# Four scale groups instead of five, and one tile's norm moved earlier, in a one-core DiT block

## Chip, cores and metric

The kernel runs on one core of a Trainium2 chip. The metric is the device time of one execution in microseconds, lower is better. Engines are named as the profile names them: PE (matrix multiply), PEld (its weight loads), DVE (vector), ACT (scalar), POOL (general purpose), SP (the queue that issues most loads).

## The reference, cut to what matters

One block of a diffusion transformer: B=2, N=256 tokens, D=1152, all bf16.

```python
mod = (silu(c) @ w_mod).reshape(B, 6, 1, D)
shift_a, scale_a, gate_a, shift_m, scale_m, gate_m = [mod[:, i] for i in range(6)]
h   = layernorm(x) * (1 + scale_a) + shift_a
q, k, v = split(h @ wqkv)                      # 2 heads
x   = x + gate_a * (softmax(q k^T / sqrt(Dh)) v @ wo)
h2  = layernorm(x) * (1 + scale_m) + shift_m
out = x + gate_m * (gelu(h2 @ w_fc1) @ w_fc2)
```

The change touches only the first line of `h` and the K projection.

## The kernel before

The start is a race between loads and PE. One SP queue loads `x`, then, in turns, a group of columns of `w_scale_a` (the scale part of w_mod) and the rows of `w_k` that go with them. PE computes the scale of a chunk of 128 channels with nine small matmuls (`scale_group`), DVE adds one to it, PE transposes the normalized chunk, DVE modulates batch 0 and ACT batch 1 (`both`), and PE does the six K matmuls of that chunk (`k_step`).

```python
SGROUPS = [(0, 2), (2, 4), (4, 6), (6, 8), (8, 9)]
for k0, k1 in SGROUPS:
    nc.sync.dma_start(w_scale_a[:, :, k0*P:k1*P], wmod_v[:, :, S_SCALE_A*D + k0*P : S_SCALE_A*D + k1*P])
    for a, z in [(0, 1), (1, 2)] if k0 == 0 else [(k0, k1)]:
        load_k(a, z, 0, KM1 * P)
# ... cut ...
for k in range(3, KD):
    split = 2 if k == 5 else 0
    k_step(k, 0, T, 0, split)                          # the first `split` of six matmuls
    if k in (3, 5, 7):
        k1 = min(k + 3, KD)
        scale_add(scale_group(k + 1, k1), k + 1, k1)
    if k < KD - 1:
        both(transpose_x([k + 1], range(NT)), k + 1)   # transposes, then modulation of step k+1
    k_step(k, 0, T, split)                             # the rest
```

Two later places matter, and the change does not touch them. After the softmax, the loads of the next weights wait for the softmax's DMA transposes, because bulk loads slow such transposes down (in the kernel before, the transpose that is issued at 87.72 us behind the load block below lands 8.9 us later; in before_piece_later, with the last 864 KB of that block held back, 4.7 us later); meanwhile POOL's queue broadcasts `gate_a` to all partitions:

```python
# inside softmax / attention output, cut
    transposed = softmaxes[i]()             # ends in nc.scalar.dma_start_transpose(...)
    if i == 0: gate_a = gate_finish()       # two gpsimd.dma_start(..., partition_broadcast(P))
# ...
w_shift_m = load_rows("w_shift_m", wmod_v, S_SHIFT_M * D)
tc.add_manual_dep(first_load["w_shift_m"], transposed.ins.name, WAIT_FOR, reason="transposes first")
w_scale_m = load_rows(...);  w_f1[0] = load_rows(...)      # the load block: 8.85 MB
w_f1[1] = wide_tile("w_f1_1")                              # first 384 columns belong to the block,
for c0, c1 in ((0, PW), (PW, D)): load = nc.sync.dma_start(w_f1[1][:, :, c0:c1], ...)
w_f1_1_rest = load.ins                                     # the rest waits for batch 1's modulation
```

And the second layernorm turns its result with DMA transposes too (`hT<-xn`, one for each token tile); DVE and ACT then modulate `hT` in place (`ln2_modulate`), and the first MLP matmul reads it.

## Time and profile before

| | before |
|---|---|
| median of 3 runs (low to high) | 244.13 us (243.77 to 244.66) |
| span of the profiled run | 242.2 us |
| PE busy, clock | 98%, 1.0 |
| first scale matmul / first Q matmul / first MLP matmul | 9.24 / 32.77 / 98.01 us |

The page of the kernel before: the span, the packets of all DMA queues, and the chain of work that ended last, by engine.

```profile
span 242.2 us, 3991 instructions
...
DMA packets 48781, 53.29 MB, mean 220 GB/s; under 512 B 9587, under 2 KB 36475, under 8 KB 48763
...
PE 85%; SPq 8%; DMA 5%; issue 0%; DVE 0%; DVEq 0%
...
```

The same chain in order of time (start us, length us, what). This is the view that says what would have to be shorter.

```profile
...
20.32 12.40 DMA w_q<-in_wqkv_dram
...
32.77 5.35 PE pq L522 x24
...
89.30 8.88 PE pacc L691 x54
98.18 68.26 PE pacc L744 x423
...
```

Up to 32.72 us the chain hangs on the load of w_q, from 32.77 us on it is PE work alone. (The chain starts a piece where the one before has ended, and pipelined ends overlap, so it has 98.18 where the timeline below has the first MLP matmul at 98.01.)

The timeline of PE in the K phase (start us, length us, engine, line, operation, out<-in, shape, count, and in brackets the idle time before it and what ended it). The start of a matmul group says more than its length, because matmuls are pipelined.

```profile
...
9.24 0.60 PE L247 MATMUL pm<-sT,w_scale_a 128*128 128x2 bf16 x18 [0.46 <-DMA w_scale_a<-in_w_mod_dram]
...
12.20 0.81 PE L280 MATMUL pk<-big,w_k 128*128 128x256 bf16 x6 [0.44 <-DVE big L270]
12.85 0.59 PE L247 MATMUL pm<-sT,w_scale_a 128*128 128x2 bf16 x18
...
15.72 0.59 PE L247 MATMUL pm<-sT,w_scale_a 128*128 128x2 bf16 x18
...
16.39 1.46 PE L280 MATMUL pk<-big,w_k 128*128 128x512 bf16 x6
...
17.91 1.89 PE L280 MATMUL pk<-big,w_k 128*128 128x512 bf16 x8
...
32.77 5.35 PE L522 MATMUL pq<-hT,w_q 128*128 128x512 bf16 x24 [0.16 <-DMA w_q<-in_wqkv_dram]
...
```

9.24 is the first scale group, just landed. 12.20 is step 0's second half (batch 1), after 0.44 us of idle PE. 12.85 is the scale of chunks 2-3, 15.72 that of chunks 4-5, ahead of step 3 (16.39). Step 4 with two matmuls of step 5 starts at 17.91. From 12.20 to 29.7 us PE has no idle time.

### The profile page before, as it was taken

The page shows a single profiled execution, that of the slowest core. Times are in us where ns is not written, and L with a number is a line of the kernel's source. Part 1 is how long each engine was busy: PE and PEld are TensorE (multiplying, and loading weights), DVE is VectorE, ACT ScalarE, POOL GpSimd, SP SyncE. Part 2 cuts the span into 40 slices and gives each one's busy share as a digit, 9 for nine tenths or more (in the row PEclk, how much of TensorE's full clock was granted, in tenths as well). Part 3 has the DMA queues.
Part 4 walks back from the last instruction along what each step waited for, and adds up shares of the span by engine and source line. Part 5 has one row for each costly group of instructions (what it writes and reads, how often), then busy time and mean ns, then how long its engine had stood idle before and what let it go on. Part 6 is the DMA issues. An engine that isn't in the chain of part 4 may idle for free.

```text
span 242.2 us, 3991 instructions
## 1 busy us (share of the span) xinstructions
PE 236.7 (98%) x1699; PEld 144.9 (60%) x1699; DVE 91.2 (38%) x193; ACT 60.0 (25%) x121; POOL 28.1 (12%) x47
## 2 busy tenths in 40 slices
PE   8899999999999999999999999999999999999994
PEld 5685444465667665888844444444666566656674
DVE  4742442318316678831001999960010000000001
ACT  6633322307215032771422233322000000000000
POOL 2200000001300333200000000001121111111111
PEclk9999999999999999999999999999999999999999
DMA  6999999997579999239999999999300000000000
GB/s 210 318 317 294 378 367 391 389 392 241 124 252 399 387 382 182 47 58 334 392 390 392 345 326 302 273 326 289 94 20 16 20 16 16 19 18 17 27 23 16
DMA packets 48781, 53.29 MB, mean 220 GB/s; under 512 B 9587, under 2 KB 36475, under 8 KB 48763
## 3 DMA queue, kind: packets, MB, share of 16 engines
q1 hardware_dynamic: 41312, 50.14, 62.4%
q10 hardware_dynamic: 6939, 1.71, 4.8%
q0 software_dynamic: 512, 1.19, 1.7%
q8 instruction: 13, 0.21, 0.4%
q14 instruction: 5, 0.04, 0.0%
HBM read 50.14 MB, written 1.19 MB: 212 GB/s over the span
## 4 chain that ended last, share of the span: by engine, by line
PE 85%; SPq 8%; DMA 5%; issue 0%; DVE 0%; DVEq 0%
PE pacc L744 29%; PE pacc L800 29%; PE pq L522 7%; PE pacc L691 7%; PE pacc L600 7%; SPq L104 5%; DMA w_q<-in_wqkv_dram 5%; PE pa L640 2%; PE ps_s L557 2%; PE pn L417 1%; SPq L107 1%; SPq L129 1%; SPq L86 1%; PE pg L499 0%; DVE tmp L806 0%
## 5 line engine op out<-in xcount | busy, mean ns | idle before, releaser
L744 PE MATMUL pacc<-hT,w_f 128*128 128x256 bf16 (+1 forms) x432 | 70.5, 326 | 0.0
L800 PE MATMUL pacc<-w_f,gT 128*128 128x384 bf16 (+2 forms) x468 | 70.5, 314 | 0.0
L800 PEld LDWEIGHTS <-gT 128*128 128x128 bf16 x468 | 44.4, 98 | 26.2
L744 PEld LDWEIGHTS <-w_f 128*128 128x128 bf16 x432 | 42.2, 98 | 27.6
L806 DVE TENSOR_TENSOR tmp<-pacc,gate 128x384 f32<-128x384 f32 (+2 forms) x13 | 6.8, 526 | 65.6 <-PE pacc L800 56.8
L776 ACT ACTIVATE gT<-pacc 128x512 bf16<-128x512 f32 x24 | 14.3, 597 | 32.6 <-PE pacc L744 32.6
L470 DVE SCALAR_TENSOR_TENSOR part<-w_gate_m,s,part 128x1152 f32<-128x1152 bf16 x16 | 21.3, 1408 | 0.0
L522 PE MATMUL pq<-hT,w_q 128*128 128x512 bf16 x81 | 17.8, 379 | 0.2 <-DMA w_q<-in_wqkv_dram 0.2
L691 PE MATMUL pacc<-w_o,big 128*128 128x384 bf16 x108 | 17.9, 326 | 0.0
L808 POOL TENSOR_TENSOR o_sb<-tmp,x 128x384 bf16<-128x384 f32 (+1 forms) x12 | 11.7, 972 | 53.8 <-DVE tmp L806 53.8
L600 PE MATMUL pacc<-w_v,hT 128*128 128x384 bf16 x108 | 17.7, 326 | 0.0
L600 PEld LDWEIGHTS <-hT 128*128 128x128 bf16 x108 | 10.5, 98 | 7.1 <-issue 0.3
L691 PEld LDWEIGHTS <-big 128*128 128x128 bf16 x108 | 10.4, 98 | 7.2 <-issue 0.4
L522 PEld LDWEIGHTS <-w_q 128*128 128x128 bf16 x81 | 7.8, 98 | 9.8 <-DMA w_q<-in_wqkv_dram 0.7
L280 PE MATMUL pk<-big,w_k 128*128 128x256 bf16 (+1 forms) x72 | 13.2, 325 | 0.4 <-DVE big L270 0.4
L697 POOL TENSOR_TENSOR x<-tmp,x_sb 128x384 f32<-128x384 f32 x8 | 7.3, 913 | 27.6 <-DVE tmp L696 27.6
L468 DVE TENSOR_SCALAR part<-w_gate_m,s 128x1152 f32<-128x1152 bf16 x2 | 1.5, 816 | 22.3 <-DMA w_gate_m<-in_w_mod_dram 22.3
L280 PEld LDWEIGHTS <-w_k 128*128 128x128 bf16 x72 | 6.8, 97 | 4.2 <-issue 0.8
L492 POOL DMA_DIRECT2D gates_dram<-nat_v x2 | 1.1, 534 | 67.5 <-DVE nat_v L490 67.5
L765 ACT ACTIVATE gT<-pacc 128x512 bf16<-128x512 f32 x12 | 6.5, 598 | 9.0 <-PE pacc L744 9.0
L513 POOL DMA_DIRECT2D gates_dram<-nat x4 | 2.3, 582 | 49.3 <-DVE nat L510 48.7
L173 PE MATMUL pwarm<-zeros 128*128 128x256 f32 x18 | 6.7, 541 | 1.2 <-DVE eps_t L93 1.2
(102 smaller groups left out, 164.8 us busy)
## 6 DMA issues: line engine op xcount, KB each, us to landing
w_f<-in_w_fc_dram SPq DMA_DIRECT2D x12, 864.0 KB, 14.8
w_f<-in_w_fc_dram SPq DMA_DIRECT2D x3, 1728.0 KB, 7.9
w_f<-in_w_fc_dram SPq DMA_DIRECT2D x2, 2592.0 KB, 17.2
w_gate_a<-in_w_mod_dram SPq DMA_DIRECT2D x3, 864.0 KB, 12.1
w_v<-in_wqkv_dram SPq DMA_DIRECT2D x3, 864.0 KB, 13.8
w_o<-in_wo_dram SPq DMA_DIRECT2D x3, 864.0 KB, 14.0
w_shift_m<-in_w_mod_dram SPq DMA_DIRECT2D x3, 864.0 KB, 6.6
w_scale_m<-in_w_mod_dram SPq DMA_DIRECT2D x3, 864.0 KB, 12.8
```

Source lines behind the costliest of these rows:

```text
L104: nc.sync.dma_start(w_k[:, k0:k1, c0:c1], wqkv_v[:, k0:k1, D + c0:D + c1])
L280: nc.tensor.matmul(pk[m][:, c0:c1], w_k[:, k, m * P:(m + 1) * P], hT0[:, k, c0:c1], start=(k == 0 and c0 == 0), stop=(k == KD - 1), skip_g ...
L470: nc.vector.scalar_tensor_tensor(part[:, b, :], wg[:, k, :], s32[:, k, b:b + 1], part[:, b, :], op0=ALU.mult, op1=ALU.add,)
L522: nc.tensor.matmul(pq[m][:], w_q[:, k, m * P:(m + 1) * P], hT[:, k, :], start=(k == 0), stop=(k == KD - 1), skip_group_check=True,)
L600: nc.tensor.matmul(pacc[:], hT[:, k, t * P:(t + 1) * P], w_v[:, k, pnl * PW:(pnl + 1) * PW], start=(k == 0), stop=(k == KD - 1),)
L691: nc.tensor.matmul(pacc[:], aT[:, k, t * P:(t + 1) * P], w_o[:, k, c0:c1], start=(k == 0), stop=(k == KD - 1),)
L697: (nc.gpsimd if pool_add else nc.vector).tensor_tensor(x1[:, t, c0:c1], tmp[:], x_sb[:, t, c0:c1], op=ALU.add)
L744: nc.tensor.matmul(dst, w_f1[m // KD][:, k, ml * P:(ml + 1) * P], hT[:, k, c0:c1], start=start, stop=(k == KD - 1), **kw,)
L776: nc.scalar.activation(gT[:, m, :], pacc[:], ACT.Gelu_apprx_tanh)
L800: nc.tensor.matmul(pacc[:], gT[:, kk, t * P:(t + 1) * P], w_f2[j][:, r, c0 - n * PW:c0 - n * PW + cw], start=(kk == 0), stop=(kk == KF - 1),)
L806: nc.vector.tensor_tensor(tmp[:], pacc[:], gate_m[:, b, c0:c0 + cw], op=ALU.mult)
L808: (nc.vector if last else nc.gpsimd).tensor_tensor(o_sb[:], tmp[:], x1[:, t, c0:c0 + cw], op=ALU.add)
```

## The change

Its intent is to shorten the K phase. Tile 3's norm moves into DVE's wait for the first scale group, so that batch 1's transposes, and with them step 0's second half, come sooner. The loads become four groups, which does away with the 256-byte rows of the last group. And scale work sits inside K steps, behind two of their six matmuls, so that its DVE and DMA waits are hidden.

```diff
--- before.py
+++ after.py
@@ -95,7 +95,7 @@
     sT = act.tile([P, KD, SW], BF16, name="sT")
     nc.gpsimd.memset(sT[:], 0.0)
 
-    SGROUPS = [(0, 2), (2, 4), (4, 6), (6, 8), (8, 9)]
+    SGROUPS = [(0, 2), (2, 4), (4, 7), (7, 9)]
     KM1 = 6
     w_scale_a = wide_tile("w_scale_a")
     w_k = wide_tile("w_k")
@@ -108,7 +108,8 @@
             w_scale_a[:, :, k0 * P:k1 * P],
             wmod_v[:, :, S_SCALE_A * D + k0 * P:S_SCALE_A * D + k1 * P],
         )
-        for a, z in [(0, 1), (1, 2)] if k0 == 0 else [(k0, k1)]:
+        ends = {0: (1, 2), 4: (5, 7)}.get(k0, (k1,))
+        for a, z in zip((k0,) + ends, ends):
             load_k(a, z, 0, KM1 * P)
     load_k(0, KD, KM1 * P, D)
 
@@ -351,31 +352,30 @@
     nc.scalar.activation(rstd1[:, 1:2], mv1[:, 1, 1:2], ACT.Ln, bias=eps_t[:], scale=1.0)
     root_exp(0, 2)
     act_stats(2)
-    stats_piece(3, 0)
-    stats_piece(3, 1)
+    for j in range(NPD):
+        stats_piece(3, j)
+    pool_eps(3)
+    pool_rsqrt(3, 4)
     norm1(1, 0, CUT)
     norm1(0, 0, CUT)
     pt_a = transpose_x([0, 1], BT[0])
-    fill(1)
-    stats_piece(3, 2)
-    pool_eps(3)
-    pool_rsqrt(3, 4)
     act_mean_eps(2)
     act_root(2)
     root_exp(2, 3)
+    norm1(3, 0, CUT)
     pm0, pm1 = [scale_group(k, k + 1, acc_tile) for k in range(2)]
     nc.vector.tensor_scalar_mul(hT0[:, 0, 0:N], pt_a[:, 0, :], pm0[:, 0, 0:1])
     nc.vector.tensor_copy(scale_a[:, 0:1, :], pm0[:])
     scale_add(pm1, 1, 2)
     modulate(pt_a, 1, 1, 0, 0, "d")
-    norm1(3, 0, CUT)
     norm1(2, 0, CUT)
+    pt_c = aux_tile([P, 2, N], "pt", BF16)
+    transpose_x([0, 1], [3], pt_c, 1)
     fill(1)
     k_step(0, 0, N)
-    k_step(1, 0, N)
-    pt_c = aux_tile([P, 2, N], "pt", BF16)
-    transpose_x([0, 1], [3], pt_c, 1)
+    k_step(1, 0, N, 0, 2)
     transpose_x([0, 1], [2], pt_c, 0)
+    k_step(1, 0, N, 2)
     modulate(pt_c, 0, 0, 1, 0, "d")
     modulate(pt_c, 1, 1, 1, 0, "a")
     norm1(0, CUT, D)
@@ -394,12 +394,12 @@
     norm1(3, CUT, D)
     k_step(2, 0, N)
     k_step(2, N, T)
+    INSIDE = {3: (2, (4, 5)), 4: (2, (5, 7)), 6: (2, (7, 9))}
     for k in range(3, KD):
-        split = 2 if k == 5 else 0
+        split, group = INSIDE.get(k, (0, None))
         k_step(k, 0, T, 0, split)
-        if k in (3, 5, 7):
-            k1 = min(k + 3, KD)
-            scale_add(scale_group(k + 1, k1), k + 1, k1)
+        if group:
+            scale_add(scale_group(*group), *group)
         if k < KD - 1:
             both(transpose_x([k + 1], range(NT)), k + 1)
         k_step(k, 0, T, split)
```

One more reading of the diff: `fill(1)`, a matmul that only keeps PE busy, occurs once less.

## The prediction

> **What bounds the kernel now.** The chain of waits that ended last is the load queue up to 32.72 us (DMA issues, then the landing of the first w_q rows), then PE without a break to the end (85% of the span, clock 1.0). So the change can gain only before 32.8 us, where PE and DMA are nearly level: in the timeline PE could start Q at about 32.43 us (K matmuls at their 0.216 us step); it starts at 32.77. The loads thus cost about 0.34 us there, and 0.1 us at the second shift section (38.05 us). Earlier PE has two idle stretches: until 9.24 us (first w_scale_a landing) and 0.44 us until 12.20 us (batch 1's first modulation).
>
> **What the change does.**
> 1. DVE: tile 3's statistics finish before the first norms, so these end near 8.45 us instead of 8.0; that hides in the wait for w_scale_a. norm1(3) (0.36 us) fits in DVE's 0.89 us wait for pm. norm1(2) ends near 10.9 instead of 11.17; with tile 3's transposes early and tile 2's after two matmuls of step 1, modulation starts near 11.3 instead of 11.80 and step 0's batch 1 near 11.7 instead of 12.20. Gain about 0.45 us (estimate). One fill goes; it sat in the 9.24 wait, worth nothing.
> 2. DMA: same bytes, but 2x1152 packets of 512 B and 1152 of 256 B become 1152 of 768 B and 1152 of 512 B. Packet durations in the trace are 18, 28, 36 ns (medians; 256, 512, 768 B), so 1152 x 10 ns / 16 engines: an estimate of 0.4-0.7 us off later landings. The Trainium skill, "DMA: Bandwidth & Descriptors", Specifications, gives 512 B as the minimum for line rate; this trace agrees in direction (14 B/ns per engine at 256 B, 18 at 512 B).
> 3. Scale groups: the same 81 small matmuls. The wider third group lands later: before near 15.2 us (issue 7.97 + 7.2), plus 1152 x 8 ns / 16 = 0.6, so 15.8, while PE now wants it near 15.7: a wait of 0-0.3 us. And transposes to the end of ACT's modulation take about 1.1 us (20.31 to 21.39), but only four matmuls of step 3 (0.87 us) cover step 4's: about 0.25 us wait, plus small ones (under 0.1) at steps 5 and 7.
>
> **Sum.** PE reaches Q at 32.43 - 0.45 + 0.1..0.5, about 32.3 us; w_q lands about 32.15 us. Q starts near 32.3 instead of 32.77 and the second shift wait (0.1 us) goes: 0.4-0.5 us gained. Everything after is PE-bound and only moves forward.
>
> Predicted: **243.7 us** (range 243.1 to 244.4, from 244.13). Chances: faster by over 2%: 0.005; within 2%: 0.99; slower: 0.005. The three runs before span 0.9 us, so the sign itself is perhaps 80% sure.
>
> **What would show it.** Page: packets under 512 B fall by 1152 from 9587. Timeline: step 0's second half near 11.7 us; first Q matmul near 32.3; second shift section near 37.5. Waits: a new wait of PE on w_scale_a or on ACT's modulation around 15-18 us. From Q on, the same PE work and length (about 206 us).
>
> **What would make it wrong.** The third group landing well after 15.8 us, or step 4's start waiting longer than 0.25 us: then w_q's earlier landing is not used. Or w_q's landing moving with one slow DMA engine rather than with the packet sum: then Q stays at 32.7.

## More of the kernel before

The timeline at the door of the MLP:

```profile
...
94.05 1.31 ACTq L682 DMA_TRANSPOSE hT<-xn  x1
...
97.55 0.60 DVE L663 TENSOR_SCALAR hT<-hT,scale_m,shift_m 128x256 bf16<-128x256 bf16 x2 [0.44 <-DMA hT<-xn]
...
98.01 1.26 PE L744 MATMUL pacc<-hT,w_f 128*128 128x256 bf16 x10
...
```

And the head of the load block, as the SP queue issues it:

```profile
...
67.73 1.43 SPq L120 DMA_DIRECT2D w_shift_m<-in_w_mod_dram  x3
...
```

The second layernorm's transpose is issued at 94.05 and DVE can start on it at 97.55. PE starts the MLP at 98.01.

## The result

| | before | after |
|---|---|---|
| first comparison, median (low to high) | 244.00 us (243.77 to 244.66), 4 runs | 244.78 us (244.36 to 244.88), 4 runs |
| second comparison, median (low to high) | 243.92 us (243.21 to 244.37), 11 runs | 244.56 us (243.65 to 245.19), 6 runs |
| span of the profiled run | 242.2 us | 243.0 us |

The ratio after/before is 1.0024 (95% interval 1.0001 to 1.0048), and 1.0023 (1.0001 to 1.0044) in the second comparison, on another occasion. A ratio here is the mean time of one kernel's fast runs over that of the other's of the same rounds, so it is not quite the ratio of the medians quoted. The change costs about 0.6 us; 0.4 us of gain had been predicted, and the measured time lies above the predicted range (243.1 to 244.4).

The page of the kernel after, the lines that answer to those of before:

```profile
span 243.0 us, 3978 instructions
...
DMA packets 47613, 53.29 MB, mean 219 GB/s; under 512 B 8419, under 2 KB 35307, under 8 KB 47595
...
PE 88%; DMA 5%; SPq 3%; DVE 1%; ACT 1%; issue 1%; DVEq 0%; ACTq 0%
...
```

Packets under 512 B fall by 1168: the 1152 predicted, and 16 four-byte ones of the load that is gone. The last line has new names: "DMA" is no longer w_q. In order of time:

```profile
...
8.00 8.13 DMA w_scale_a<-in_w_mod_dram
...
32.96 5.18 PE pq L522 x24
...
94.07 4.21 DMA hT<-xn
...
98.38 0.36 DVE hT L663
...
98.78 23.95 PE pacc L744 x217
...
```

The load of w_q has left the chain. In its place stands the landing of the third scale group (8.13 us up to 16.13), and far behind it, at 94.07, a DMA transpose of the second layernorm. The 24 Q matmuls take 5.18 us, 0.216 us each. The Trainium skill, "TensorE: Matmul & The Clock Gate", section "Back-to-back issue gap", gives N/2.4 + 2.5 ns for an isolated matmul, which is 216 ns for 512 columns, and about 131 ns for such matmuls in a stream of weight loads and matmuls. The Q matmuls are such a stream, with one weight load each, and the trace agrees with the formula and not with the figure for streams. PE's own work is not what changed: in the timelines these 24 take 5.35 us before and 5.34 after.

PE in the K phase after, and one line of its weight loads (the second fence), which shows a wait that the matmul view hides:

```profile
...
9.36 0.60 PE L248 MATMUL pm<-sT,w_scale_a 128*128 128x2 bf16 x18 [0.31 <-DMA w_scale_a<-in_w_mod_dram]
...
11.37 1.42 PE L281 MATMUL pk<-big,w_k 128*128 128x256 bf16 x10
12.63 0.59 PE L248 MATMUL pm<-sT,w_scale_a 128*128 128x2 bf16 x18
...
16.17 0.38 PE L248 MATMUL pm<-sT,w_scale_a 128*128 128x2 bf16 x9 [0.30 <-DMA w_scale_a<-in_w_mod_dram]
...
16.63 1.73 PE L281 MATMUL pk<-big,w_k 128*128 128x512 bf16 x6
18.20 0.59 PE L248 MATMUL pm<-sT,w_scale_a 128*128 128x2 bf16 x18
...
32.80 5.34 PE L522 MATMUL pq<-hT,w_q 128*128 128x512 bf16 x24
...
```

```profile
...
17.77 0.10 PEld L281 LDWEIGHTS <-w_k 128*128 128x128 bf16 x1 [0.39 <-issue]
...
```

Chunks 2-3's scale starts 3.27 us after the first scale matmul (12.63 - 9.36), where it was 3.61 (12.85 - 9.24): the early norm works. Then PE waits at 16.17 for the third load, and its weight load at 17.77 (step 4) for the modulation: the profile names no releaser ("issue"), but ACT's half of that modulation ends at 17.71, and the kernel before has no such wait at step 4. At Q, PE arrives at 32.80 and does not wait at all: the whole gain is gone, though w_q landed at 30.71.

The door of the MLP after:

```profile
...
94.07 1.31 ACTq L682 DMA_TRANSPOSE hT<-xn  x1
...
98.38 0.61 DVE L663 TENSOR_SCALAR hT<-hT,scale_m,shift_m 128x256 bf16<-128x256 bf16 x2 [1.25 <-DMA hT<-xn]
...
98.78 0.49 PE L744 MATMUL pacc<-hT,w_f 128*128 128x256 bf16 x3 [0.58 <-DVE hT L663]
...
```

And the head of the load block:

```profile
...
68.19 1.43 SPq L121 DMA_DIRECT2D w_shift_m<-in_w_mod_dram  x3
...
```

The transpose is issued at the same time (94.07) but lands 0.8 us later, and PE, which was done, waits 0.58 us. From the first MLP matmul to the end both profiles have the same length: 242.2 - 98.01 and 243.0 - 98.78 are both 144.2 us.

So the trace of the changed kernel names two candidates: the K phase, and a landing 60 us later, in code that nobody touched. One of them could be chance. That is what the experiments had to settle.

### The profile page after: what moved, and what is told of

It is laid out like the page before. It is cut to its first block, busy times and chain, and to the rows that moved or that the text cites. A ratio compares the mean times of both kernels' runs of the same rounds, so it can differ in the third digit from the quotient of the medians.

```text
span 243.0 us, 3978 instructions
## 1 busy us (share of the span) xinstructions
PE 236.7 (97%) x1687; PEld 145.1 (60%) x1698; DVE 91.5 (38%) x193; ACT 60.2 (25%) x121; POOL 28.3 (12%) x47
## 4 chain that ended last, share of the span: by engine, by line
PE 88%; DMA 5%; SPq 3%; DVE 1%; ACT 1%; issue 1%; DVEq 0%; ACTq 0%
PE pacc L800 29%; PE pacc L744 29%; PE pacc L600 7%; PE pq L522 7%; PE pacc L691 4%; DMA w_scale_a<-in_w_mod_dram 3%; PE pk L281 3%; PE pk L310 2%; SPq L104 2%; DMA hT<-xn 2%; PE pa L640 2%; PE ps_s L557 2%; PE pn L417 2%; SPq L86 1%; PE pm L248 1%
## 5 line engine op out<-in xcount | busy, mean ns | idle before, releaser
L808 POOL TENSOR_TENSOR o_sb<-tmp,x 128x384 bf16<-128x384 f32 (+1 forms) x12 | 11.7, 973 | 53.4 <-DVE tmp L806 53.4
L600 PEld LDWEIGHTS <-hT 128*128 128x128 bf16 x108 | 10.5, 98 | 7.1 <-issue 0.3
L174 PE MATMUL pwarm<-zeros 128*128 128x256 f32 x18 | 7.4, 586 | 1.2 <-DVE eps_t L93 1.2
```

The costliest lines, as they stand in the source:

```text
L174: nc.tensor.matmul(dst[:, 0:T // 2], zeros32[:, 0:P], zeros32, start=True, stop=True)
L600: nc.tensor.matmul(pacc[:], hT[:, k, t * P:(t + 1) * P], w_v[:, k, pnl * PW:(pnl + 1) * PW], start=(k == 0), stop=(k == KD - 1),)
L808: (nc.vector if last else nc.gpsimd).tensor_tensor(o_sb[:], tmp[:], x1[:, t, c0:c0 + cw], op=ALU.add)
```

## Experiments

### How to read the table

Fifteen further runs were made in four batches, two of them of the two kernels as they are. For each profile, five times are enough. A is the start of the first scale matmul of w_scale_a, B that of chunks 2-3's scale, Q the first Q matmul, I the issue of w_shift_m (head of the load block behind the softmax transposes), M the first MLP matmul. The undisturbed PE path from Q to M is 65.24 us, the least that any profile shows to within 0.01; the last column is what M - Q has above it.

| run | A | B - A | Q - B | Q - A | I - Q | wait before M |
|---|---|---|---|---|---|---|
| before (first profile) | 9.24 | 3.61 | 19.92 | 23.53 | 34.96 | 0 |
| before_again | 9.55 | 3.61 | 19.60 | 23.21 | 34.63 | 0 |
| before_fewer_issues | 9.26 | 3.61 | 19.59 | 23.20 | 32.83 | 0 |
| order_only | 9.27 | 3.31 | 19.60 | 22.91 | 32.79 | 0 |
| order_fewer_issues | 9.59 | 3.31 | 19.60 | 22.91 | 34.89 | 0 |
| inside_old_loads | 8.87 | 3.54 | 19.94 | 23.48 | 35.00 | 0.18 |
| after (first profile) | 9.36 | 3.27 | 20.17 | 23.44 | 35.39 | 0.74 |
| after_again | 9.69 | 3.32 | 20.15 | 23.47 | 35.17 | 0 |
| after_more_issues | 8.99 | 3.44 | 20.01 | 23.45 | 35.18 | 0.26 |
| groups_only | 9.27 | 3.61 | 19.91 | 23.52 | 35.44 | 0.39 |
| wide_last | 9.16 | 3.36 | 19.64 | 23.00 | 35.17 | 0.49 |
| wide_last_more_issues | 9.71 | 3.09 | 19.83 | 22.92 | 35.31 | 0.52 |
| before_gate_late | 9.47 | 3.61 | 19.59 | 23.20 | 32.68 | 0.70 |
| after_gate_late | 9.63 | 3.08 | 20.41 | 23.49 | 32.70 | 0 |
| before_piece_later | 9.11 | 3.62 | 19.58 | 23.20 | 34.50 | 0 |
| after_piece_later | 9.51 | 3.29 | 20.16 | 23.45 | 35.37 | 0 |
| order_piece_later | 9.66 | 3.34 | 19.59 | 22.93 | 34.49 | 0 |

A wanders between 8.87 and 9.71 us although the first loads of all these kernels are the same, about as much as the kernel before spreads over its timed runs (0.9 us), and it is why only differences are compared. In inside_old_loads A came so early that B waited for the norms and not for A; there only Q - B is of use. Where B came early after A with the new loads (3.08, 3.09), Q - B grows by as much, since PE then waits longer for a load: Q - A of the five profiles of the changed kernel and its variants stays within 23.44 to 23.49.

### First batch: what is chance, and which half costs

**before_again**: no edit.

> The unchanged kernel, as a control. Two theories of the 0.6 us that the changed kernel lost at the start of the first MLP matmul (98.78 us instead of 98.18): by chance, the landing of the last softmax transposes (and with it the issue of the next loads, 67.73 against 68.19 us) varies from run to run; or the change causes it. If by chance, this second profile of the same kernel may show an issue of those loads between 67.6 and 68.4 us, different from 67.73; if by the change, it stays within 0.1 us of 67.73 (both relative to a first Q matmul at 32.77). Ratio to the kernel before: 1.000 within 0.2%.

Measured: ratio 1.0008 (0.9993 to 1.0023), so two names of one kernel differ by nothing clear. Its PE timeline:

```profile
...
9.55 0.60 PE L247 MATMUL pm<-sT,w_scale_a 128*128 128x2 bf16 x18 [0.82 <-DMA w_scale_a<-in_w_mod_dram]
...
13.16 0.59 PE L247 MATMUL pm<-sT,w_scale_a 128*128 128x2 bf16 x18
...
32.76 5.34 PE L522 MATMUL pq<-hT,w_q 128*128 128x512 bf16 x24
...
```

There is no wait for w_q: the first scale group came 0.31 us later than in the first profile, PE was later by that, and Q still starts at 32.76. Q - A is 23.21, not 23.53. And w_q's first rows landed at 32.04, not at 32.72. The wait for w_q on which the prediction had built was one execution's. The loads behind the softmax transposes were issued at 67.39, 0.34 us before the first profile's 67.73: chance moves this time, as the first theory had it, but see the last batch.

**after_again**: no edit.

> The changed kernel once more. Ratio 1.002 (the first comparison gave 1.0024). First Q matmul at 32.8 within 0.15 us in both theories, since the waits before it (third scale group landing at 16.1, step 4's modulation) are set by fixed work. Issue of the loads behind the softmax transposes: near 68.2 again if the change causes the delay, anywhere in 67.6 to 68.4 if it is chance.

Measured: ratio 1.0023. First Q matmul at 33.16, outside the expected 0.15 us, because A was later by 0.33; Q - A is 23.47 against 23.44. Issue of the loads at 68.33 us, no wait before M. So the changed K phase is slower by 0.26 us each time, and the wait before M comes and goes.

**order_only**: the change without its groups.

```diff
 # against the changed kernel
-    SGROUPS = [(0, 2), (2, 4), (4, 7), (7, 9)]
+    SGROUPS = [(0, 2), (2, 4), (4, 6), (6, 8), (8, 9)]
 # and the loop over k from 3 on as in the kernel before
```

> Only the norm and transpose order of the change, with the old five scale groups. My theory: PE gains 0.2 to 0.3 us by the second scale group (12.53 us in the changed kernel instead of 12.75), keeps it to the end of the K matmuls, and then gives it back waiting for the first w_q rows, whose landing stays near 32.7 because the packets are as before: first Q matmul at 32.7 to 32.8, a wait for w_q of 0.3 to 0.6 us before it, ratio 1.000. Rival (the reordering itself is what costs): ratio 1.002, first Q matmul after 32.9.

Measured: ratio 1.0002 (0.9981 to 1.0022).

```profile
...
9.27 0.60 PE L247 MATMUL pm<-sT,w_scale_a 128*128 128x2 bf16 x18 [0.30 <-DMA w_scale_a<-in_w_mod_dram]
...
12.58 0.59 PE L247 MATMUL pm<-sT,w_scale_a 128*128 128x2 bf16 x18
...
32.18 5.34 PE L521 MATMUL pq<-hT,w_q 128*128 128x512 bf16 x24
...
```

The gain of 0.30 us at B is there and is kept to Q. The expected wait for w_q is not: Q starts at 32.18, so w_q had landed by then even with the old packets. My theory of a fixed landing near 32.7 falls here. The rival (the order costs) falls too. The time shows no clear gain; its interval includes the 0.3 us.

**groups_only**: the loads and the inside places, on the kernel before.

```diff
 # against the kernel before
-    SGROUPS = [(0, 2), (2, 4), (4, 6), (6, 8), (8, 9)]
+    SGROUPS = [(0, 2), (2, 4), (4, 7), (7, 9)]
+    INSIDE = {3: (2, (4, 5)), 4: (2, (5, 7)), 6: (2, (7, 9))}   # and the changed loop
```

> Only the new scale groups, with the old norm and transpose order. My theory: third group still lands near 16.1 us and PE wants it near 16.05, so nearly no wait there, but step 4's wait for the modulation (0.3 to 0.4 us) stays; PE reaches Q at 32.7 to 32.9 without waiting for w_q, which lands before 32.5. Ratio 1.000 to 1.002. Rival (only the wider group's late landing costs): first Q matmul at 32.4 to 32.5 and ratio 0.999 or less.

Measured: ratio 1.0032 (1.0013 to 1.0050), the clearest loss of the batch.

```profile
...
12.88 0.59 PE L248 MATMUL pm<-sT,w_scale_a 128*128 128x2 bf16 x18
...
16.18 0.37 PE L248 MATMUL pm<-sT,w_scale_a 128*128 128x2 bf16 x9
...
32.79 5.34 PE L523 MATMUL pq<-hT,w_q 128*128 128x512 bf16 x24
...
```

Its weight loads, of which one waits at step 4 as in the changed kernel:

```profile
...
17.76 0.10 PEld L281 LDWEIGHTS <-w_k 128*128 128x128 bf16 x1 [0.39 <-issue]
...
```

As expected PE shows no DMA wait at 16.18, and Q comes at 32.79. (The weight load before it does wait 0.24 us for the third load, but chunk 4's scale starts 3.30 us after B, against 3.29 in inside_old_loads below, where the load is early.) Q - B is 19.91, 0.31 us above 19.60: that is the new places of the scale work by themselves, step 4's thin cover first of all. And there is a wait of 0.39 us before M. The groups carry the loss, the order does not.

### Second batch: the two costs of the K phase, and the gate broadcast

**inside_old_loads**: the changed kernel with the five old loads. It separates the third load's late landing from the places of the scale work.

```diff
 # against the changed kernel
-    SGROUPS = [(0, 2), (2, 4), (4, 7), (7, 9)]
+    SGROUPS = [(0, 2), (2, 4), (4, 6), (6, 8), (8, 9)]
```

> The changed kernel's order and its scale work inside steps 3, 4 and 6, but the five old loads. This takes the late landing of the third load away and leaves the thin cover of step 4. Theory with both terms: no DMA wait before chunk 4's scale (near 15.9 us), a PE wait of 0.3 us before step 4, first Q matmul near 32.5, that is half of the 0.6 us between the order alone (32.18) and the full change (32.80). Rival A (only the landing matters): 32.2. Rival B (only the placement): 32.8.

Measured: first Q matmul at 32.35, with a first scale matmul 0.4 us earlier than order_only's.

```profile
...
12.41 0.59 PE L247 MATMUL pm<-sT,w_scale_a 128*128 128x2 bf16 x18
...
15.70 0.37 PE L247 MATMUL pm<-sT,w_scale_a 128*128 128x2 bf16 x9
...
32.35 5.34 PE L521 MATMUL pq<-hT,w_q 128*128 128x512 bf16 x24
...
```

```profile
...
17.29 0.10 PEld L280 LDWEIGHTS <-w_k 128*128 128x128 bf16 x1 [0.39 <-issue]
...
```

No wait for the load, the same wait of a weight load at step 4, and Q - B is 19.94: 0.34 us above the old places, close to groups_only. The full change has 20.01 to 20.41 (mean of its five profiles 20.18), so the landing costs another 0.1 to 0.5 us, 0.24 on average over five profiles, against this one without it. Both terms show in the profiles. The timed runs were two near 243.7 and four from 245.2 to 246.9 us (ratio 1.0046, 1.0004 to 1.0088). The profile is one of the quick ones. The slowest run has a clock of 0.993 (one run of before in this batch, 245.73 us, has 0.992); three others near 245.4 have the full clock, and what happened in them is not known.

**wide_last**: the order, with the merge put into the last load.

```diff
 # against order_only
-    SGROUPS = [(0, 2), (2, 4), (4, 6), (6, 8), (8, 9)]
+    SGROUPS = [(0, 2), (2, 4), (4, 6), (6, 9)]
-        if k in (3, 5, 7):  k1 = min(k + 3, KD)
+        if k in (3, 5):     k1 = 6 if k == 3 else KD
```

> The reordered norms, with loads 0-1, 2-3, 4-5, 6-8 (the 256 B group merged into the last one instead of into the third), and scale work where the kernel before has it: chunks 4-5 ahead of step 3, 6-8 inside step 5. Theory: the merge itself is harmless where PE does not stand at the door: third group wanted near 15.4 us and there by 15.4, last wanted near 19.4 and landing near 19.2; first Q matmul near 32.2 as in the run with the order alone (32.18), ratio 0.999 to 1.000. Rival (four groups cost wherever): first Q matmul after 32.6.

Measured: Q at 32.16 as expected, so in the K phase the merge is harmless there. But the time missed: ratio 1.0032 (1.0003 to 1.0062). Its profile, the quickest of its six runs (243.91 us), waits 0.49 us before M; the others were not profiled, so this wait may be only part of the miss. So here a late loss comes with the new loads though the K phase is quick.

**before_gate_late** and **after_gate_late**: the gate broadcast waits for the softmax transposes.

```diff
-            gate_a = gate_finish()
+            gate_broadcast = gate_finish()
+        if i == len(softmaxes) - 1:
+            gate_a = gate_broadcast(transposed)   # both loads get a WAIT_FOR on the last transpose
```

> The kernel before, with one wait added: the gate_a broadcast (two 288 KB loads from POOL's queue) starts only when the last softmax transposes have landed. Theory (contention): so far those transposes end 4.4 to 5 us after their issue because their last small packets stand behind the broadcast; without it the loads of w_shift_m are issued near 65 us instead of 67.4 to 67.7, the load block ends some 2 us earlier, and the first MLP matmul stays PE-bound at 65.24 us after the first Q matmul in every run. Time: 0.999 to 1.000 of before. Rival (the transposes are slow by themselves): issue stays at 67 to 68.

> The changed kernel with the same added wait. If the late landing is half of the changed kernel's loss: loads issued near 65 us, first MLP matmul 65.24 us after the first Q matmul (it was 65.98 in the first profile), ratio to before 1.000 to 1.001 instead of 1.0023, what is left being the K phase. Rival (all of the loss lies in the K phase): ratio stays at 1.002.

Measured: ratios 0.9990 (0.9961 to 1.0019) and 1.0013 (0.9984 to 1.0043), neither clear. The loads are issued at 65.35 and 65.82 us, 2 us sooner, so the broadcast does hold up the last softmax transpose. The Trainium skill, "DMA: Bandwidth & Descriptors", section "Issuing engines are not separate DMA queues", says that loads issued by different engines run on the same 16 DMA engines and interleave; this run agrees, for a load of POOL's queue moved the landing of a transpose of ACT's by 2 us. But it bought nothing. At the MLP's door of before_gate_late:

```profile
...
93.94 1.31 ACTq L686 DMA_TRANSPOSE hT<-xn  x1
...
98.21 0.60 DVE L667 TENSOR_SCALAR hT<-hT,scale_m,shift_m 128x256 bf16<-128x256 bf16 x2 [1.21 <-DMA hT<-xn]
...
98.61 0.60 PE L748 MATMUL pacc<-hT,w_f 128*128 128x256 bf16 x4 [0.55 <-DVE hT L667]
...
```

(This profile is of the slowest of its six runs, 244.56 us.) DVE starts on hT at 98.21, 65.54 us after Q, later than in before (64.78): the broadcast now overlaps the head of the load block (its packets run from 70.0 to 73.9 us), and the block takes 31.8 us from its first issue to its last landing, against 28.5 in before. In after_gate_late it takes 30.5 us, and M does not wait. Moving one transfer behind another on busy DMA engines changed who waits. The theory that the sooner issue would free the MLP's start in every run was wrong.

### Third batch: less to load in front of the MLP

Here the last 864 KB of the load block are held back until the second layernorm's first transposes have landed. They are not needed before about 107 us.

```diff
+    f1_1_loads = []
     for c0, c1 in ((0, PW), (PW, D)):
         load = nc.sync.dma_start(w_f1[1][:, :, c0:c1], wfc1_v[:, :, D + c0:D + c1])
-    w_f1_1_rest = load.ins
+        f1_1_loads.append(load.ins)
+    w_f1_1_first, w_f1_1_rest = f1_1_loads
 # in ln2_normalize
-            ln2_modulate(0, k, eng)
+            mod = ln2_modulate(0, k, eng)
+            if k == 0:
+                tc.add_manual_dep(w_f1_1_first, mod.ins.name, WAIT_FOR, reason="transposes first")
```

> The kernel before, with the last 864 KB of the load block ahead of the first MLP matmul (columns 0 to 383 of w_f1_1, not needed before about 107 us) held back until the first batch's normalized transposes have landed. Theory: the first MLP matmul starts at the later of two times, 65.24 us after the first Q matmul (PE) and 0.4 us after the landing of those transposes, which wait for the end of the load block; with 0.88 MB less (2.3 us at 390 GB/s) the transposes land 1.5 to 2.3 us earlier, near 95.5, and the start is PE-bound: 65.24 after Q in the profile. Time 0.998 to 1.000 of before, since only some of its runs are held by the transposes. Rival (the landing is set by something else than the load block): landing stays near 97.4.

> The changed kernel with the same piece held back. Theory: the wait before the first MLP matmul (0.6 us in its first profile) is gone, first Q matmul still 23.4 to 23.7 us after the first scale matmul (before: 23.2), so 0.3 us slower than the kernel before with the same piece held back, a difference of ratios of about 0.0012. Rival (the whole loss of the change lay behind Q): equal to the kernel before with the piece held back.

> The order alone (old loads, old places of the scale work) with the piece held back: the gain of 0.3 to 0.5 us at Q can now reach the end. First Q matmul 22.9 us after the first scale matmul or at the landing of w_q; first MLP matmul 65.24 us after Q. Ratio to before 0.997 to 0.999, and about 0.0025 below the changed kernel with the same piece held back. Rival (a gain before Q is always lost later): 1.000.

Measured: 0.9988 (0.9975 to 1.0000), 1.0006 (0.9992 to 1.0020) and 0.9986 (0.9974 to 0.9999) of before. The door of before_piece_later:

```profile
...
93.59 1.31 ACTq L686 DMA_TRANSPOSE hT<-xn  x1
...
96.89 0.60 DVE L665 TENSOR_SCALAR hT<-hT,scale_m,shift_m 128x256 bf16<-128x256 bf16 x2 [0.24 <-DMA hT<-xn]
...
97.55 1.69 PE L748 MATMUL pacc<-hT,w_f 128*128 128x256 bf16 x14
...
```

In all three profiles DVE starts on hT 64.57 to 64.60 us after Q, and there is no wait before M. Without the hold-back that figure runs from 64.61 to 65.58. The expected landing near 95.5 was a miss: once the load block is out of the way, the transpose still takes 3.3 us from issue (93.59) to DVE's start. But the figure no longer wanders, and it lies below 64.84, which is 65.24 less the 0.40 us between DVE's start and M in the profiles that waited. Of these three kernels only the changed one had ever waited without the hold-back, and that in one of its two profiles, so these three alone would prove little. But the landing of the block's last piece sorts all 14 profiles without the hold-back: it comes 63.79 to 64.75 us after Q in the seven that wait before M, and 61.54 to 63.41 us in the seven that do not. So the load block is what makes M late, by when it ends, and the profiles fit the rule: M starts at the later of Q + 65.24 and DVE's start on hT + 0.40.

With the wait gone, changed and unchanged kernel still differ by 1.0006 - 0.9988 = 0.0018, or 0.4 us, with intervals that overlap; Q - A (23.45 against 23.20) accounts for 0.25 of it. So the rival (all the loss lies behind Q) falls, by Q - A more than by these times. order_piece_later is the best version here in the middle, but not clearly better than before_piece_later: the 0.27 us that it has at Q is less than these runs can tell apart.

### Fourth batch: is it the number of load issues?

By now all kernels with four scale loads and the gate broadcast in its old place had issued the load block 35.17 to 35.44 us after Q, and all with five loads 32.79 to 35.00. The slowest packet of the gate broadcast, read from the packets of the trace, took 0.83 to 1.04 us in the former and 0.51 to 0.75 us in the latter. Four scale loads also mean one load issue fewer. These four kernels turn that count around, with w_gate_a in two or four pieces instead of three, and leave the early loads alone.

```diff
-    w_gate_a = load_rows("w_gate_a", wmod_v, S_GATE_A * D)
+    w_gate_a = load_rows("w_gate_a", wmod_v, S_GATE_A * D, (0, 3, 6, 7, 9))   # more_issues
+    w_gate_a = load_rows("w_gate_a", wmod_v, S_GATE_A * D, (0, 6, 9))         # fewer_issues
```

> The changed kernel with one load issue more: w_gate_a in four pieces instead of three, so the SP queue has issued as many loads as in the kernel before; all packets as in the changed kernel. Open point: in all five profiles of kernels with four scale loads, the loads behind the softmax transposes are issued 35.2 to 35.4 us after the first Q matmul and the slowest packet of the gate broadcast takes 0.83 to 1.04 us; in all six with five scale loads it is 32.8 to 35.0 us and 0.51 to 0.75 us. If the number of issues is what matters, this run shows under 35.05 us and under 0.8 us; if the packet sizes or the order of the early loads, 35.2 or more and over 0.8 us.

> The kernel with loads 0-1, 2-3, 4-5, 6-8 and w_gate_a in four pieces. Number of issues: under 35.05 us from first Q matmul to the issue of the loads and slowest gate packet under 0.8 us. Packet sizes: 35.2 or more and over 0.8 us.

> The kernel before with w_gate_a in two pieces instead of three, so one load issue fewer, as in the changed kernel; early loads as before. Number of issues: 35.2 us or more from the first Q matmul to the issue of the loads, slowest gate packet over 0.8 us. Packet sizes: under 35.05 and under 0.8.

> The order alone with w_gate_a in two pieces. Number of issues: 35.2 us or more, slowest gate packet over 0.8 us. Packet sizes: under 35.05 and under 0.8. First Q matmul 22.9 us after the first scale matmul in both.

Measured, I - Q and slowest gate packet: 35.18 us and 1.05 us; 35.31 and 0.84; 32.83 and 0.86; 34.89 and 0.49. On I - Q all four say "early loads, not the number of issues", the first by only 0.01 to 0.02 us. On the slowest packet three of four do; before_fewer_issues has 0.86 us. There, as in order_only (0.72 us), the broadcast was issued 1.12 and 0.90 us after the last softmax transpose, not 0.62 to 0.66 as in the others; the transpose landed in 2.4 us, not 4.2 to 5.2, and the broadcast ran into the load block. So before_fewer_issues says little about the number of issues. The ratios to before were 1.0018, 1.0024, 1.0002 and 1.0013, of two runs each, all unclear.

So, with the gate broadcast in its old place, seven profiles with four early loads stand at 35.17 us or more, and eight with five at 35.00 or less (34.49 to 35.00 without the two just named). Chance alone would hardly sort them so. But the block's start does not by itself say when it ends: in the ten of these profiles that have neither a piece held back nor a late broadcast (the two just named), it takes between 28.2 and 29.4 us from first issue to last landing. How loads that end before 25 us make a broadcast at 65 us slower, no view shows. This stays open.

## Why the prediction was wrong, point by point

1. **The norm order (step 1): right in kind, too large.** Predicted 0.45 us at step 0's second half; measured at B, 0.30 us (3.61 to 3.31). Step 0's second half, expected near 11.7, starts at 11.98 (12.20 before). Tile 2's norm did not start near 10.5 us but at 10.78, after its root had come from ACT at 10.69, and it ended at 11.19, no sooner than before (11.17; expected near 10.9).
2. **The packets (step 2): the count was right, there was nothing to gain.** Packets under 512 B fell as predicted, and packet durations still read 18, 28 and 36 ns in the kernel before (medians). The Trainium skill, "DMA: Bandwidth & Descriptors", section "Why small descriptors are slow (HBM only)", explains such figures by a fixed cost for each packet, and these durations agree in that 256 B more cost 8 to 10 ns each while the first 256 B cost 18. But the step that failed is "The loads thus cost about 0.34 us there, and 0.1 us at the second shift section". That was the wait of one execution, in which w_q's first rows landed at 32.72 us, the latest of nine profiles with the old loads (the other eight: 30.48 to 32.04). In before_again, before_fewer_issues and before_piece_later PE starts Q 23.20 to 23.21 us after A without a wait, in the last two with A as early as in the first profile (9.26 and 9.11). The eight profiles with four loads have w_q sooner, at 29.88 to 30.87, but sooner loads at Q are worth nothing when PE is not there to use them. The 0.1 us at the second shift section was not gained either: it starts 5.28 us after Q before and 5.27 after.
3. **Scale groups (step 3): right in kind, a little too small.** Predicted 0 to 0.3 us for the third load and 0.25 us for step 4, with under 0.1 more at later steps; the sum took 0.1 to 0.5 us for all of it. Measured: 0.1 to 0.5 us (mean 0.24) and 0.31 to 0.34 us, together 0.57; the second was seen alone twice. With the 0.30 us of point 1 the K phase comes out at -0.30 + 0.33 + 0.24 = +0.27 us; Q - A shows 23.46 against 23.20, +0.26.
4. **"Everything after is PE-bound and only moves forward": this failed.** In the first profile of before, DVE started on hT at 97.55, so hT held the MLP back to 97.95, and PE came at 98.01: a margin of 0.06 us, which the chain of waits does not show, because it follows only the one that came last. In the changed kernel the wait behind it was 0.74, 0 and 0.26 us (after, after_again, after_more_issues), 0.33 on average, against 0 in before, before_again and before_fewer_issues. So the step left out the second path to M: the loads and transposes can arrive after PE.

The sum of 3 and 4, 0.27 + 0.33 = 0.60 us, fits the measured 0.0023 x 244 = 0.56 us; but the second term is a mean of three profiles from 0 to 0.74, and the interval of the measured loss goes from 0.02 to 1.07 us, so the fit is no test. Shown: both K phase terms, in the profiles (groups_only, inside_old_loads), and that the end of the load block sets the wait before M (its landings in 14 profiles, and the piece held back). Likely, from one profile of each kernel: that the early loads and not the issue count go with its later start (fourth batch). Not shown: by what path the early loads reach it, what share of the wait before M comes from its later start and what share from its varying length, and why four timed runs of inside_old_loads were slow.

## What to carry to other kernels

A wait that one trace shows at the seam of two nearly level streams is one draw from a distribution: profile the unchanged kernel twice before you credit a change with removing it. Before you write "from here on only engine X counts", look at every join behind the change for the margin of the stream that came second. And merging loads to have fewer small packets moves the landing of everything in the merged load to its end; merge where the consumer is late, not where it stands at the door, and do not place dependent work where fewer matmuls are left than its latency (here 0.87 us of matmuls for 1.1 us of transposes and modulation).

## What the Trainium skill lacked or had wrong

- "DMA: Bandwidth & Descriptors" (Specifications, "Why small descriptors are slow (HBM only)"): the trace agrees that small packets are slow, but 512 B, the page's minimum for line rate, is not yet line rate here (medians in the kernel before, up to 33 us: 18 B/ns per engine at 512 B, 24.5 at 2304 B), and its account of small rows does not weigh the other side, that a merged load gives its first chunk only when all of it has landed. ("Perfetto Trace Analysis", section "DMA Optimizations", does name splitting as a way to start sooner.) Here the third group landed at 16.13 us, and PE, ready some tenths sooner, waited: 0.24 us on average.
- "DMA: Bandwidth & Descriptors" (sections "DMA Transpose (X-bar)" and "Issuing engines are not separate DMA queues"): neither says what a transpose costs behind a running load block. Here the same transpose took about 3.3 us from issue to use with the last 864 KB held back, and 3.3 to 4.3 us without; the one issued 6.3 us before it landed in 4.7 to 7.1 us with the piece held back, and in 7.4 to 9.7 us without.
- "Perfetto Trace Analysis": I found nothing in it on the spread between executions of one kernel. Here the first load's landing moved the first scale matmul from 8.87 to 9.71 us over profiles, more than the whole effect under study.
- "TensorE: Matmul & The Clock Gate" (section "Back-to-back issue gap"): its figure of about 131 ns for a stream of 512-column matmuls does not hold here; the 24 Q matmuls step at 216 ns.
- I found no page on why early load shapes would change the speed of a broadcast 40 us later (I - Q at 35.17 to 35.44 us in seven profiles against 32.79 to 35.00 in eight); the cause is open.
